# Layer 1's third couple: seven factor products over two pairs in place of eight block products, with the weight preparation moved ahead

## Chip, cores and metric

One Trainium2 chip, one core. The metric is the device time of one execution in microseconds (us), median of three runs. All matrix data is fp32; the kernel splits each operand into a high part (the value rounded to fp32r by a copy) and a low part (the rest) and forms each product as high·high + low·high + high·low, so three matmuls stand for one.

## What is computed

```
kv  = einsum('bhsd,bhse->bhde', k, v)            # 8 batches, 8 heads, 576 tokens, width 64
out = einsum('bhsd,bhde->bhse', q, kv)
x   = out / sqrt(mean(out^2) + 1e-6) * g_norm     # -> (4608, 512)
h   = x @ w_in;  x = (h * sigmoid(1.702 h)) @ w_out        # layer 1: 512 -> 2048 -> 512
h   = x @ w_in2; y = (s * relu(h)^2 + b) @ w_out2          # layer 2: 512 -> 2048 -> 512
```

## The kernel before

The 4608 tokens are nine tiles of 512; the 2048 hidden units are sixteen slices f of 128. Layer 1 of tiles 0, 1 and 2 runs first, in 48 "steps" (tile, f), by plain products: `mm1` (L587) makes one slice of h with 12 matmuls, `mm2` (L615) adds its share of the output two steps later with 12 more. Beside the steps, attention for later tiles is computed, layer 1's weights are unpacked from 64-bit words (`to_f32`, L155) and split, and `prep_first(p)` (L248) makes the weight factors that the next stage needs for w_in, from two slices at a time. It is a generator; `make()` advances it by one piece, three times at the end of each step (L1503), and one starts every fourth step from step 10 (L1196).

Then tiles go in couples of 1024 tokens: couples 0, 1, 2 are layer 1 of tiles 3 to 8, couples 3 to 6 are layer 2 of tiles 0 to 7, and tile 8 of layer 2 is last and alone. A couple has eight "pairs" P of two slices f; pairs 0 to 23 are layer 1, 24 to 55 layer 2. The first product of a pair is seven factor products i = 0 to 6 (`product`, L682; a "tick" is one of them), whose results are combined on the scalar and vector engines (`after`, L766).

The second product is done in two ways. In layer 1 `units` (L808) does, for each pair, eight block products ("unit": one token half t and one output block c) of six matmuls over 512 columns; the half t = 1 goes through a PSUM bank that the vector engine adds into SBUF (`z`, L840; one bank until pair 13, then two, L820), the half t = 0 stays in PSUM. The units of pair P-1 run between the products of pair P. In layer 2 a "quad" is two pairs: `quad_unit` (L974) does seven factor products in two halves h, one at each tick of the following two pairs, each of 12 matmuls over 256 columns; `factor_add`, `factor_hi` and `factor_lo` (L937, L959, L967) make the seven factors, `combine` (L1010) puts the results of a couple together when it has ended, and `load_t` (L867) loads the weight factors that `prep_out` (L270) stored. In the first two pairs of layer 2 no quad is there yet, so PE has only layer 1's last units and the first products.

Layer 2's weights are unpacked (`convert2`, L557) and turned into factors (`prep_in`, `prep_out`, L289 and L270) during the couples, as two tasks of a planner: at each tick `background` (L1250) advances tasks whose due tick has come, and others while the counted time of the vector and scalar engines leaves room. The due ticks are `14 + made2*4.6` and `18 + made2*4.6` (L1244), so the 32 slices end at about tick 161, pair 23. `parts_hl` (L225) splits a factor in a staging tile (`wst0`, `wst1`) and stores it to DRAM; `spaced` keeps two ticks between two of them.

All DMAs of these stages stand in SP's queue, in the order of the program.

Of the kernel before, what the change touches and what calls it, by code (L numbers as in the profile page):

```python
# [16 lines left out]
P = 128  # L17
# [27 lines left out]
ROOM = 500.0  # L45

# [6 lines left out]
def tile_attn_moe_moe2(  # L53
# [101 lines left out]
    def to_f32(which, ph, f):  # L155

        raw = w_raw.pop((which, ph, f))
        lo, hi = raw[:, :, 0], raw[:, :, 1]  # L160
        w = rot("wf", 3, (P, DM), U32)
# [58 lines left out]
    def spaced():  # L220
        while couples_on and now[0] < stored[0] + 2:
            yield 1
        stored[0] = now[0]

    def parts_hl(dst, src, n):  # L225

        yield
        yield from spaced()
# [4 lines left out]
        if isinstance(dst, list):  # L233
            for x, part in enumerate(dst):
                move(part, t[:, x])
        else:
            move(dst, t)
# [29 lines left out]

    wt_dram = {}

    def prep_out(p):  # L270

        wa, wb = (w_raw.pop((1, 1, f)) for f in (2 * p, 2 * p + 1))
        if p == 0:
            wt_dram.update({x: dp.tile([P, 8, 2, 2, KP], F32, name=f"wt{x}") for x in range(KF // 4)})
        a, b = (x.rearrange("p (h e) -> p h e", h=2) for x in (wa, wb))
        d = wt_dram[p // 2][:, :, p % 2]
        c = new("wc", (P, 4, KP))
        tt = vector.tensor_tensor
# [5 lines left out]
        yield from parts_hl(d[:, 0:8:7], a, 2)  # L284
        yield from parts_hl(d[:, 1:3], c[:, 0:2], 2)
        yield from parts_hl(d[:, 3:5], c[:, 2:4], 2)
        yield from parts_hl(d[:, 5:7], b, 2)

    def prep_in(p):  # L289
        a, b = (w_raw.pop((0, 1, f)).rearrange("p (h e) -> p h e", h=2) for f in (2 * p, 2 * p + 1))  # L290
        d = wi_dram[1, p] = dp.tile([P, 8, 2, KP], F32, name=f"wi1_{p}")
        c = new("wc", (P, 4, KP))
        yield from sums_of(a, b, c)
        yield from parts_hl(d[:, 0:2], a, 2)
        yield from parts_hl(d[:, 2:4], c[:, 0:2], 2)
        yield from parts_hl(d[:, 4:6], c[:, 2:4], 2)
        yield from parts_hl([d[:, 7], d[:, 6]], b, 2)
# [235 lines left out]
    def split_x(s, i):  # L533

        lay, m, _ = couples[s]
        if i == 6 and s > first2:
# [18 lines left out]
    made2 = [0, 0]  # L555

    def convert2():  # L557

        for m, (which, f) in enumerate(order2):
            made2[0] = m  # L560
            while m >= made2[1] + 3:
                yield 1
            for n, _ in enumerate(to_f32(which, 1, f)):
                yield 1 if n == 0 else 0
            if m + 2 < len(order2):
                load_w(order2[m + 2][0], 1, order2[m + 2][1])
        made2[0] = len(order2)

    def prepare2():

        for m, (which, f) in enumerate(order2):
# [4 lines left out]
            yield from (prep_in, prep_out)[which](f // 2)  # L576
            made2[1] = m + 1
# [69 lines left out]
    P2 = first2 * (KF // 2)  # L647
    place_of = {}
# [53 lines left out]

    def width(P_):
        return couples[pairs[P_][0]][1]

    raws = {}
    def c_new(P_, e):

        if layer(P_):
            q_, m = (P_ - P2) // 2, width(P_)  # L710
# [33 lines left out]
    def g_hi(P_, e):  # L744

        if layer(P_):
            return
# [12 lines left out]
    def g_lo(P_, e):  # L760
        if layer(P_):
            return
# [96 lines left out]
    FACTORS = 7  # L859
# [3 lines left out]
    quads = [(s_, x) for s_ in range(first2, LAST) for x in range(KF // 2 // BY)]  # L863
    t_t, f_t, mid_t, m_ps, m_sb = {}, {}, {}, {}, {}
    t_next = [0]

    def load_t():  # L867
# [3 lines left out]
        if n < len(quads) * FACTORS:  # L871
            q_, k_ = divmod(n, FACTORS)
            t = t_t[q_, k_] = new(f"wo{n % T_RING}", (P, 2, 2, KP), F32R)
            move(t, wt_dram[quads[q_][1]][:, k_])
        elif n < len(quads) * FACTORS + KF - 2:
            load_last(n - len(quads) * FACTORS, f"wo{n % T_RING}")

    def load_last(f, tag):
        t = t_t["last", f] = new(tag, (P, 2, 2, KP), F32R)
        move(t, wt_dram[f // 4][:, (slice(0, 8, 7), slice(5, 7))[f % 2], f // 2 % 2])  # L880
# [93 lines left out]
    def quad_unit(q_, k_, h):  # L974
# [13 lines left out]
        for c in range(2):  # L988
# [21 lines left out]
    def combine(s, h):  # L1010
# [4 lines left out]
        def send(k_, t, right):  # L1015
            row = js[0] * BT + t * m + 2 * h * P
# [49 lines left out]
    def load_wo2():  # L1066
# [4 lines left out]
        if n < first2 * KF:  # L1071
# [86 lines left out]
    for x, slot in ((0, 2), (0, 2), (0, 5), (0, 5), (1, 5)):  # L1158
        at((P2 + x, slot), "load", load_t)
# [35 lines left out]
    for p in range(KF // 2):  # L1195
        todo.setdefault(10 + 4 * p, []).append((prep_first, p))  # L1196
# [9 lines left out]
    for m in range(2):  # L1206
        at(len(steps) - 3 + m, "raw", load_w, 0, 1, m)
# [16 lines left out]
    def plan():  # L1224
# [3 lines left out]
        for s_ in range(len(couples)):  # L1228
            n0 = n * s_
            need = []  # L1230
            if s_:
                if couples[s_][0]:
                    need = [Task(y_get(s_), n0 - n + 6, n0 - n + 7)]
                if s_ < LAST:
                    need = [Task(fac_sums(s_), n0 - (14 if s_ <= first2 else 35), n0 - 9, need)]
            for i in range(7 if s_ < LAST else 2):
                if (s_, i) in split_early:
                    continue
                more = [split[s_, 1]] if (i == 6 and s_ <= first2 and (s_, 1) in split) else []
                split[s_, i] = Task(split_x(s_, i), max(0, n0 - 7 + i + 1), max(0, n0 + i - (4 if i < 6 else 5)), need + more)  # L1240
            if first2 <= s_ < LAST:
# [17 lines left out]
    with tc.manual_schedule():  # L1259
# [204 lines left out]

        split_early = [(0, i) for i in range(4)]
# [6 lines left out]
        for n in range(FIRST, N1):  # L1472
            conv = to_f32(*convs.pop(n)) if n in convs else iter(())
            start(n)
            run(n, "splith")
# [9 lines left out]
            run(n, "pe")  # L1485
            next(conv, None)
# [7 lines left out]
            next(conv, None)  # L1494
            y_out(n - 2, 2)
# [7 lines left out]
            make()  # L1503
            make()
            make()
            if n == N1 - 5:
                load_half(0)
# [38 lines left out]
        for P_, (s_, p) in enumerate(pairs):  # L1546
            lay, m, js = couples[s_]
            for i in range(7):
# [4 lines left out]
                at_q = ((P_ - P2) // BY, 7 * (P_ % BY) + i)  # L1553
                after(P_, i)
                if lay:
# [16 lines left out]
                elif i == 2 and layer(P_ - 1) == 0:  # L1572
                    running.append(units(P_ - 1))
                for _ in range({6: 2}.get(i, 1) if P_ < P2 else 1 if P_ == P2 or i % 2 == 0 else 0):
# [3 lines left out]
                if lay:  # L1578
# [3 lines left out]
                background(tick, slot, SLACK, ROOM if lay and P_ > P2 + 1 else 9999.0)  # L1582
# [87 lines left out]
```

## Time and profile before

| | |
|---|---|
| median of three runs | 1584.61 us (1583.83 to 1585.3) |
| the profiled execution, its own time | 1585.22 us |
| span of its profile | 1583.5 us |
| TensorE (PE) busy | 1563.4 us, 99% |
| VectorE (DVE), ScalarE (ACT) busy | 1001.3 us, 63% and 937.4 us, 59% |
| moved by DMA | 372.71 MB, mean 235 GB/s |

Engines are PE (matmul), PEld (its weight loads), DVE, ACT, POOL and SP. PE's busy time counts pipelined matmuls whose shown duration (0.39 us) is longer than their spacing, so the time of a stretch is read from start to start. The steps lie at 26 to 323 us of the span, pairs 0 to 15 at 323 to 682, pairs 16 to 23 at 682 to 846, layer 2's pairs 24 and 25 at 846 to 879, its other pairs up to 1471, and the lone tile at the end.

### The profile page before, as it was taken

The numbers are of one execution on the slowest core, as the hardware profiler recorded it, in microseconds if no ns is written. First come the engines' busy times: TensorE is split into PE (matmuls) and PEld (weight loads), VectorE is DVE, ScalarE is ACT, GpSimd is POOL, SyncE is SP. The second block draws the span as 40 slices with busy tenths as digits, with TensorE's granted clock in tenths as the row PEclk, the third lists the DMA queues.
The fourth block names the chain that finished last, engine by engine and source line by source line (L and its number), as shares of the span: only waits on it lengthen the run. The fifth ranks groups of instructions, "written<-read, shape, count | busy, mean of one in ns | idle before, by whom it ended". The sixth has DMA issues, their size and how long they took to land.

```text
span 1583.5 us, 23132 instructions
## 1 busy us (share of the span) xinstructions
PE 1563.4 (99%) x8880; PEld 1338.7 (85%) x8880; DVE 1001.3 (63%) x1478; ACT 937.4 (59%) x1520; POOL 69.3 (4%) x49
## 2 busy tenths in 40 slices
PE   7999999999999999999999999999999999999999
PEld 6788888878887888888888899899999998999987
DVE  6877743456666666777885466866686668556620
ACT  4766643454445555464446866776677677766652
POOL 4000111101000010000000000000000000000000
PEclk9999999999999999999999999999999999999999
DMA  8678877567776876789975755685568556755563
GB/s 279 199 265 308 274 259 258 199 207 244 272 240 231 293 255 219 248 278 362 357 282 199 253 188 186 213 268 189 185 216 263 188 188 210 241 193 184 189 219 113
DMA packets 127039, 372.71 MB, mean 235 GB/s; under 512 B 12626, under 2 KB 29266, under 8 KB 119762
## 3 DMA queue, kind: packets, MB, share of 16 engines
q1 hardware_dynamic: 126786, 371.12, 69.6%
q8 instruction: 70, 1.15, 0.3%
q14 instruction: 39, 0.32, 0.1%
q10 hardware_dynamic: 144, 0.13, 0.0%
HBM read 289.41 MB, written 81.79 MB: 234 GB/s over the span
## 4 chain that ended last, share of the span: by engine, by line
PE 90%; DVE 5%; ACT 2%; DMA 2%; issue 1%; SPq 0%; POOL 0%; DVEq 0%; ACTq 0%; POOLq 0%
PE A L696 6%; PE A L697 6%; PE A L698 6%; PE m L995 4%; PE m L994 4%; PE m L993 4%; PE D L696 3%; PE D L697 3%; PE D L698 3%; PE sum L830 3%; PE sum L832 3%; PE sum L831 3%; PE acc L624 3%; PE acc L625 3%; PE z L830 3%; PE acc L626 3%
## 5 line engine op out<-in xcount | busy, mean ns | idle before, releaser
L995 PE MATMUL m<-wo,fac 128*128 128x256 f32 x640 | 180.8, 283 | 0.6 <-DVE fac L89 0.6
L994 PE MATMUL m<-wo,fac 128*128 128x256 f32 x640 | 180.7, 282 | 0.0
L993 PE MATMUL m<-wo,fac 128*128 128x256 f32 x640 | 180.0, 281 | 0.0
L89 ACT ACTIVATE gh<-gh 128x512 f32<-128x512 f32 x72 | 45.4, 632 | 145.3 <-DVE gh L89 145.2
L994 PEld LDWEIGHTS m<-wo,fac 128*128 128x128 f32 x640 | 122.2, 191 | 6.1
L993 PEld LDWEIGHTS m<-wo,fac 128*128 128x128 f32 x640 | 121.2, 189 | 7.0
L995 PEld LDWEIGHTS m<-wo,fac 128*128 128x128 f32 x640 | 121.2, 189 | 1.2 <-DVE fac L89 1.2
L696 PE MATMUL A<-wi,xl 128*128 128x512 f32 x296 | 117.5, 397 | 1.9 <-ACT ev L89 0.7
L697 PE MATMUL A<-wi,xl 128*128 128x512 f32 x296 | 116.2, 393 | 0.0
L698 PE MATMUL A<-wi,xl 128*128 128x512 f32 x296 | 115.2, 389 | 0.0
L89 DVE TENSOR_TENSOR madd<-m,madd 128x512 f32<-128x512 f32 x122 | 83.8, 688 | 49.4 <-PE m L995 49.4
L89 ACT ACTIVATE wraw<-wraw 128x512 uint32<-128x512 uint32 (+1 forms) x128 | 82.7, 646 | 52.6 <-DVE wraw L89 52.6
L425 POOL TENSOR_TENSOR r<-ms,mhalf 128x8 f32<-128x8 f32 x36 | 65.6, 1826 | 544.0 <-DVE ms L89 543.9
L89 DVE TENSOR_TENSOR fac<-s,fac 128x1024 fp32r<-128x1024 f32 x64 | 77.9, 1218 | 15.0 <-ACT fac L89 15.0
L89 ACT ACTIVATE g<-h 128x512 f32<-128x512 f32 x52 | 31.0, 597 | 79.8 <-PE h L598 69.6
L596 PE MATMUL h<-xh,wi 128*128 128x512 f32 x192 | 76.5, 399 | 1.2 <-ACT g L89 1.2
L830 PE MATMUL z<-wo,wo 128*128 128x512 f32 x192 | 76.1, 396 | 1.2 <-DVE g L89 0.7
L624 PE MATMUL acc<-gh,wo 128*128 128x512 f32 x192 | 76.7, 399 | 0.0
L625 PE MATMUL acc<-gh,wo 128*128 128x512 f32 x192 | 75.1, 391 | 0.7 <-DVE wo L89 0.7
L626 PE MATMUL acc<-gl,wo 128*128 128x512 f32 x192 | 75.0, 390 | 0.0
L598 PE MATMUL h<-xl,wi 128*128 128x512 f32 x192 | 74.9, 390 | 0.0
L832 PE MATMUL z<-wo,wo 128*128 128x512 f32 x192 | 74.9, 390 | 0.0
(264 smaller groups left out, 4370.7 us busy)
## 6 DMA issues: line engine op xcount, KB each, us to landing
wo<-wt SPq DMA_DIRECT2D x127, 512.0 KB, 4.0
wo<-wo SPq DMA_DIRECT2D x80, 512.0 KB, 5.1
xl<-wi SPq DMA_DIRECT2D x37, 1024.0 KB, 6.5
xl<-wi SPq DMA_DIRECT2D x37, 768.0 KB, 5.9
wi<-wst SPq DMA_DIRECT2D x40, 512.0 KB, 4.5
xh<-wi SPq DMA_DIRECT2D x19, 1024.0 KB, 6.7
wraw<-in_w_in SPq DMA_DIRECT2D x32, 512.0 KB, 4.1
wraw<-in_w_out SPq DMA_DIRECT2D x32, 512.0 KB, 4.4
```

What stands on the lines that cost most here:

```text
L89: return fn(*args, **kw)
L624: nc.tensor.matmul(o, wh[:, ds_], gh, start=(f == lo), stop=False)
L625: nc.tensor.matmul(o, wl[:, ds_], gh, start=False, stop=False)
L626: nc.tensor.matmul(o, wh[:, ds_], gl, start=False, stop=(f == hi - 1))
L696: nc.tensor.matmul(o, wh, xh, start=(c == 0 and not more), stop=False, skip_group_check=more)
L697: nc.tensor.matmul(o, wl, xh, start=False, stop=False, skip_group_check=more)
L698: nc.tensor.matmul(o, wh, xl, start=False, stop=(c == 1), skip_group_check=more)
L830: nc.tensor.matmul(o, wh[:, cs], gh, start=begins, stop=False)
L832: nc.tensor.matmul(o, wh[:, cs], gl, start=False, stop=ends)
L993: nc.tensor.matmul(o[:, c, :], hi[:, y, cs], w[:, y, 0, :], start=begins, stop=False)
L994: nc.tensor.matmul(o[:, c, :], hi[:, y, cs], w[:, y, 1, :], start=False, stop=False)
L995: nc.tensor.matmul(o[:, c, :], lo[:, y, cs], w[:, y, 0, :], start=False, stop=ends)
```

## The change

- Couple 2 (pairs 16 to 23) does its second product in quads. Four quads of layer 1 come before the sixteen of layer 2. A layer 1 factor product has the weights standing and the 512 tokens moving: six matmuls over 512 columns for each half h. `c_new`, `g_hi`, `g_lo`, `factors`, `beside_quads` and `combine` take these pairs as they took layer 2's; the two pairs without a quad are now 16 and 17.
- `prep_first_out(p)`, eight of them from step 33 on, make the w_out factors for layer 1 and store them. `prep_first` starts at steps 10, 14, 18, 21, 24, 26, 28, 30; from step 21 `make()` is called four times in a step, two of them in its middle.
- Layer 2's weight preparation: the first raw loads six steps earlier; 14 advances of `convert2` in steps 41 to 47; then due ticks by small steps, `7 + (steps2[0]-15)*0.66` and `8 + steps2[1]*0.68`, so it ends at about tick 106, pair 15. Converting may be four slices ahead (three before).
- Staging: the stores leave at the next tick; a staging tile may be taken again after three ticks, at most one a tick, and `f5` is a third tile in ticks 4 to 40 and 60 to 96.
- The planner's room for DVE is 1300 ns a tick up to pair 17 (9999 before), 500 after.
- Couple 3 makes its seventh factor in places of its own, as couples 4 to 6 do, and its sums may start earlier.

```diff
+REUSE = 3
+F5_TAKEN = ((-99, 3), (41, 59), (97, 999))
...
-        t = rot("wst", 2, (P, 2, 2, KP), F32R)[:, 0:n]
+        t = (yield from staging())[:, 0:n]
...
-            move(dst, t)
+        stores.append((dst, t))
+        if not couples_on and not 33 <= now[0] < len(steps) - 5:
+            store()
...
+    def prep_first_out(p):
+        if p % 2 == 0:
+            wt_dram[0, p // 2] = dp.tile([P, FACTORS, 2, 2, KP], F32, name=f"wt0_{p // 2}")
+        d = wt_dram[0, p // 2][:, :, p % 2]
+        ab = new("f5", (P, 2, 2, KP))
+        for x in range(2):
+            parts = [part.rearrange("p (h e) -> p h e", h=2) for part in w_out[0, 2 * p + x]]
+            for y, part in enumerate(parts):
+                if x == 0:
+                    move(d[:, 0, y, :], part[:, 0, :])
+                else:
+                    move(d[:, 5:7, y, :], part)
+            vector.tensor_tensor(out=ab[:, x], in0=parts[0].bitcast(F32), in1=parts[1].bitcast(F32), op=ALU.add)
+        yield
+        c = new("wc", (P, 4, KP))
+        yield from out_sums(ab[:, 0], ab[:, 1], c)
+        yield from parts_hl(d[:, 1:3], c[:, 0:2], 2)
+        yield from parts_hl(d[:, 3:5], c[:, 2:4], 2)
...
-            while m >= made2[1] + 3:
+            while m >= made2[1] + 4:
...
+    firstq = first2 - 1
+    PQ = firstq * (KF // 2)
...
-    quads = [(s_, x) for s_ in range(first2, LAST) for x in range(KF // 2 // BY)]
+    quads = [(s_, x) for s_ in range(firstq, LAST) for x in range(KF // 2 // BY)]
...
+        for y in range(BY) if couples[s][0] == 0 else ():
+            hs = slice(h * P, (h + 1) * P)
...
+            nc.tensor.matmul(flat, w[:, y, 0, hs], hi[:, y, :], start=begins, stop=False)
+            nc.tensor.matmul(flat, w[:, y, 1, hs], hi[:, y, :], start=False, stop=False)
+            nc.tensor.matmul(flat, w[:, y, 0, hs], lo[:, y, :], start=False, stop=ends)
...
-        todo.setdefault(10 + 4 * p, []).append((prep_first, p))
+        todo.setdefault((10, 14, 18, 21, 24, 26, 28, 30)[p], []).append((prep_first, p))
+    for p in range(KF // 2):
+        todo.setdefault(33 + 7 * p // 4, []).append((prep_first_out, p))
...
-        at(len(steps) - 3 + m, "raw", load_w, 0, 1, m)
+        at(len(steps) - 9 + m, "raw", load_w, 0, 1, m)
...
-        Task(convert2(), 7, lambda: 14 + made2[0] * 4.6)
-        Task(prepare2(), 5, lambda: 18 + made2[1] * 4.6)
+        Task(converting, 6, lambda: 7 + (steps2[0] - 15) * 0.66)
+        Task(prepare2(), 7, lambda: 8 + steps2[1] * 0.68)
...
+            if n >= N1 - 7:
+                for _ in range(2):
+                    next(converting)
...
-                background(tick, slot, SLACK, ROOM if lay and P_ > P2 + 1 else 9999.0)
+                background(tick, slot, SLACK, ROOM if P_ > PQ + 1 else 1300.0)
```

## Rows read from the trace of the kernel before

**Rows 1.** The page: busy time of the engines, and the chain that ended last.
```profile
PE 1563.4 (99%) x8880; PEld 1338.7 (85%) x8880; DVE 1001.3 (63%) x1478; ACT 937.4 (59%) x1520; POOL 69.3 (4%) x49
PE 90%; DVE 5%; ACT 2%; DMA 2%; issue 1%; SPq 0%; POOL 0%; DVEq 0%; ACTq 0%; POOLq 0%
```
**Rows 2.** Windows by stage: from:to, us, busy of each engine, clock, DMA share, GB/s.
```profile
224.30:280.60 56.30, 55.13 (x378) 45.41 (x376) 18.75 (x36) 19.29 (x37) 8.82 (x5) 1.00 0.75 248
280.60:322.60 42.00, 42.00 (x203) 34.97 (x201) 17.81 (x25) 18.50 (x32) 6.20 (x3) 1.00 0.59 202
322.60:501.40 178.80, 176.20 (x950) 142.68 (x949) 115.97 (x196) 91.41 (x166) 14.63 (x8) 1.00 0.71 239
501.40:682.30 180.90, 179.78 (x905) 147.30 (x904) 124.60 (x212) 93.57 (x169) 13.82 (x8) 1.00 0.75 256
682.30:845.50 163.20, 163.20 (x721) 135.14 (x721) 128.61 (x204) 83.08 (x146) 0.00 (x0) 1.00 0.85 308
845.50:879.00 33.50, 32.85 (x145) 26.85 (x144) 13.53 (x17) 20.60 (x33) 0.00 (x0) 1.00 0.72 262
1018.30:1451.00 432.70, 432.31 (x2769) 392.61 (x2768) 284.75 (x333) 306.67 (x453) 0.00 (x0) 1.00 0.65 214
```
**Rows 3.** PE's timeline: first matmuls of two units 512 columns wide.
```profile
727.23 0.39 PE L830 MATMUL sum<-wi,wo 128*128 128x512 f32 x1
...
729.95 0.39 PE L830 MATMUL z<-wo,wo 128*128 128x512 f32 x1
```
**Rows 4.** PE's timeline: a layer 2 factor product, and the matmul after it.
```profile
1060.84 0.28 PE L993 MATMUL m<-wo,fac 128*128 128x256 f32 x1
...
1062.27 0.40 PE L696 MATMUL A<-wi,xl 128*128 128x512 f32 x1
```
**Rows 5.** What PE waited for, 320 to 682 us: total us, times, longest.
```profile
PE xtp L435 <- DVE xn L89: 0.8, 2, 0.6
PE z L830 <- DVE g L89: 0.7, 2, 0.6
PE A L696 <- ACT ev L89: 0.7, 1, 0.7
```
**Rows 6.** What PE waited for, whole span: layer 2's start, quads, mm2.
```profile
PE acc L625 <- DVE wo L89: 0.7, 2, 0.5
...
PE A L696 <- ACT wst L89: 0.7, 1, 0.7
PE m L995 <- DVE fac L89: 0.6, 3, 0.2
```
**Rows 7.** Groups by line, whole span: weight preparation on DVE and ACT.
```profile
L89 DVE TENSOR_SCALAR wf<-wf 128x512 f32<-128x512 f32 (+1 forms) x128 | 54.1, 423 | 13.4 <-ACT wf L89 12.3
...
L89 DVE TENSOR_TENSOR wst<-wc,wst 128x512 fp32r<-128x512 f32 x48 | 32.5, 685 | 2.1 <-ACT wst L89 2.1
...
L89 ACT CAST wst<-wc 128x512 fp32r<-128x512 f32 x48 | 29.6, 616 | 12.5 <-DVE wc L89 5.4 <-DMA wt<-wst 3.9 <-DMA y<-ev 1.7
...
L89 DVE TENSOR_TENSOR wc<-wf 128x256 f32<-128x256 f32 x32 | 13.3, 417 | 0.0
```
**Rows 8.** Windows, DVE on wf tiles alone: pairs 0 to 15, 16 to 23.
```profile
322.60:682.30 359.70, 74.22 (x144) 1.00 0.73 248
682.30:845.50 163.20, 41.37 (x80) 1.00 0.85 308
```
**Rows 9.** Windows, all engines: steps 24 to 28.
```profile
166.60:198.20 31.60, 31.37 (x154) 26.08 (x153) 22.57 (x43) 19.98 (x36) 4.12 (x2) 1.00 0.80 273
```
**Rows 10.** Windows, all engines: pair 18.
```profile
723.10:743.50 20.40, 20.40 (x91) 16.89 (x91) 12.95 (x24) 10.57 (x20) 0.00 (x0) 1.00 1.01 394
```
**Rows 11.** DMA issues from 682 to 800 us: KB each, median us to landing.
```profile
f<-y SPq DMA_DIRECT2D x15, 512.0 KB, 7.6
```
**Rows 12.** DMA issues from 322 to 682 us: stores of staged factors.
```profile
wt<-wst SPq DMA_DIRECT2D x20, 512.0 KB, 3.8
```
**Rows 13.** What SP's queue waited for, 320 to 682 us.
```profile
SPq L125 <- DVE wst L89: 103.9, 29, 8.3
```

More of the change, by code (lines that the diff above doesn't have):

```diff
@@ L218, in tile_attn_moe_moe2, with staging @@
     now, stored = [0], [-9]
-    def spaced():
-        while couples_on and now[0] < stored[0] + 2:
+    used = {"wst0": -99, "wst1": -99, "f5": -99}
+    def staging():
+        if not couples_on:
+            turns["wst"] = turns.get("wst", -1) + 1
+            places = ("wst0", "xh1", "xl1") if 33 <= now[0] < len(steps) - 5 else ("wst0", "wst1")
+            return new(places[turns["wst"] % len(places)], (P, 2, 2, KP), F32R, "wst")
+        while True:
+            free = [x for x in used if now[0] - used[x] >= REUSE and (x != "f5" or not any(lo <= now[0] <= hi for lo, hi in F5_TAKEN))]
+            if free and now[0] > stored[0]:
+                x = min(free, key=used.get)
+                used[x] = stored[0] = now[0]
+                return new(x, (P, 2, 2, KP), F32R, "wst")
             yield 1
-        stored[0] = now[0]
     def parts_hl(dst, src, n):
         yield
-        yield from spaced()
-        t = rot("wst", 2, (P, 2, 2, KP), F32R)[:, 0:n]
+        t = (yield from staging())[:, 0:n]
         scalar.copy(t[:, :, 0, :], src)
@@ L232, in parts_hl, with store @@
         vector.tensor_tensor(out=t[:, :, 1, :], in0=src, in1=t[:, :, 0, :].bitcast(F32), op=ALU.subtract)
[L233 to L236, printed above, removed]
-            move(dst, t)
+        stores.append((dst, t))
+        if not couples_on and not 33 <= now[0] < len(steps) - 5:
+            store()
+    stores = []
+    def store():
+        while stores:
+            dst, t = stores.pop(0)
+            if isinstance(dst, list):
+                for x, part in enumerate(dst):
+                    move(part, t[:, x])
+            else:
+                move(dst, t)
     def sums_of(a, b, c):
@@ L575, in prepare2 @@
                 continue
-            yield from (prep_in, prep_out)[which](f // 2)
-            made2[1] = m + 1
+            for wait in (prep_in, prep_out)[which](f // 2):
+                steps2[1] += wait != 1 or stored[0] == now[0]
+                yield wait
     steps = [(j, f, lo, hi) for j, lo, hi in PARTS for f in range(lo, hi)]
@@ L701, in layer, with quad @@
         return couples[pairs[P_][0]][0]
+    def quad(P_):
+        return P_ >= PQ
     def width(P_):
@@ L707, in c_new @@
     def c_new(P_, e):
-        if layer(P_):
-            q_, m = (P_ - P2) // 2, width(P_)
+        if quad(P_):
+            q_, m = (P_ - PQ) // 2, width(P_)
             if (q_, e) not in raws:
@@ L744, in g_hi @@
     def g_hi(P_, e):
-        if layer(P_):
+        if quad(P_):
             return
@@ L760, in g_lo @@
     def g_lo(P_, e):
-        if layer(P_):
+        if quad(P_):
             return
@@ L858, in tile_attn_moe_moe2 @@
     BY = 2
-    FACTORS = 7
     T_RING = 5
@@ L987, in quad_unit @@
             o = m_ps[key]
-        for c in range(2):
+        for y in range(BY) if couples[s][0] == 0 else ():
+            hs = slice(h * P, (h + 1) * P)
+            begins = y == 0 and (first or not held(q_, k_))
+            ends = y == BY - 1 and (last or not held(q_, k_))
+            flat = o.rearrange("p a b -> p (a b)")
+            nc.tensor.matmul(flat, w[:, y, 0, hs], hi[:, y, :], start=begins, stop=False)
+            nc.tensor.matmul(flat, w[:, y, 1, hs], hi[:, y, :], start=False, stop=False)
+            nc.tensor.matmul(flat, w[:, y, 0, hs], lo[:, y, :], start=False, stop=ends)
+        for c in range(2) if couples[s][0] else ():
             cs = slice((2 * h + c) * P, (2 * h + c + 1) * P)
@@ L1156, in tiles_in @@
             at((P_, 3 * e + 3), "pre", x_raw, i + e)
-    for x, slot in ((0, 2), (0, 2), (0, 5), (0, 5), (1, 5)):
-        at((P2 + x, slot), "load", load_t)
+    for x, slot in ((0, 2), (0, 2), (0, 5), (1, 4), (1, 5)):
+        at((PQ + x, slot), "load", load_t)
     at(n0 + 10, "load", load_q, 5 * TT)
@@ L1485, in tile_attn_moe_moe2 @@
             run(n, "pe")
+            for _ in range(0 if n < 21 else 1):
+                make()
             next(conv, None)
@@ L1494, in tile_attn_moe_moe2 @@
             next(conv, None)
+            for _ in range(0 if n < 21 else 1):
+                make()
             y_out(n - 2, 2)
@@ L1502, in tile_attn_moe_moe2 @@
             run(n, "load")
-            make()
-            make()
-            make()
+            for _ in range(3 if n < 21 else 2):
+                make()
+            if n >= N1 - 7:
+                for _ in range(2):
+                    next(converting)
             if n == N1 - 5:
+                store()
                 load_half(0)
@@ L1571, in tile_attn_moe_moe2 @@
                             y_out(N1 - 1, d)
-                elif i == 2 and layer(P_ - 1) == 0:
+                elif i == 2 and not quad(P_ - 1):
                     running.append(units(P_ - 1))
-                for _ in range({6: 2}.get(i, 1) if P_ < P2 else 1 if P_ == P2 or i % 2 == 0 else 0):
+                for _ in range({6: 2}.get(i, 1) if P_ < PQ else 1 if P_ == PQ or i % 2 == 0 else 0):
                     while running and next(running[0], StopIteration) is StopIteration:
```

57 lines of the change are left out of this document (38 added, 19 removed), and 2 rows, old and new, of the table PLACES.

## Prediction

> **What bounds the kernel now.** I read the page first. PE is busy for 99% of the span, and the chain that ended last runs through PE for 90% [rows 1]. So the time is PE's work plus the few microseconds in which it waits, and a change pays only by taking matmuls away or gives back by making PE wait. Next the timeline, for what a matmul costs: from the first matmul of a unit at 727.23 to that of the unit after next at 729.95 lie twelve matmuls 512 columns wide, 2.72 us, 0.2267 us each [rows 3]. Then the windows: pairs 16 to 23 last 163.2 us, 20.40 a pair [rows 2]. A pair has 42 matmuls of first products and 48 of units, and 90 x 0.2267 = 20.40: in couple 2 PE loses nothing at all today. Last the waits: in pairs 0 to 15 PE waited on DVE and ACT for little more than these 2.2 us [rows 5], and elsewhere behind the start for single ones, DVE's `wo`, ACT's `wst` and DVE's `fac` [rows 6]. The reader is to see a PE that is full, with a DVE that is busy 65%, 69% and 79% of pairs 0 to 7, 8 to 15 and 16 to 23 [rows 2].
>
> **The second product of couple 2.** Removed: 8 pairs x 8 units x 6 = 384 matmuls of 512 columns. Added: 4 quads x 7 factors x 2 halves x 6 = 336 of the same width. So 48 x 0.2267 = 10.9 us leave PE [rows 3]. A pair should go from 20.40 to 84 x 0.2267 = 19.04 us. For a check from another shape, layer 2's factor half takes 1.43 us for twelve matmuls of 256 columns [rows 4], and its pairs 432.7 / 22 = 19.67 us [rows 2]; the wide form, six at 0.2267 = 1.36 us, is a little cheaper. [...]
>
> **The edge.** The two pairs without a quad last 33.5 us today [rows 2], for 144 matmuls = 32.6, with one wait of 0.7 us on ACT [rows 6]. They move from 24 and 25 to 16 and 17 with the same content: 0. Pairs 24 and 25 then carry the last layer 1 quad and `combine`. Layer 2's couples pay at this place one wait each, three in all for 0.6 us, on DVE's `fac` [rows 6]; with the slowing that follows I add 0.4 us, between 0 and 1.
>
> **DVE in pairs 16 to 25.** Out go 32 additions of z, 32 low parts of g and the preparation; in come, per quad, four additions and seven low parts on 1024 elements and ten additions from PSUM. Layer 2 has the same load and DVE is busy 66% there [rows 2], with these small waits; ACT has no squares to make in layer 1. The fetching of couple 3's four partial sums stays here with its due ticks. I take 0 for it, and 2 us as the worst.
>
> **The preparation, moved ahead.** On wf tiles DVE spent 74.2 us in pairs 0 to 15 and 41.4 in 16 to 23 [rows 8]; `wst<-wc` adds two thirds of 32.5 = 21.7 us in all [rows 7], 7.8 of them late in the same proportion. So 49 us come forward. Some 6 us of it (14 advances, not three slices, at 2 x 0.42 + 2 x 0.69 us) go to steps 41 to 47; 43 us are added to the 240.6 us of pairs 0 to 15, which makes 284 of 359.7 us, 79% [rows 2, 7]. That is just what DVE had in pairs 16 to 23, where PE lost nothing [rows 2]. But from pair 13 z has two banks and before that one, with a single product of 1.36 us between two z units: there a late DVE stops PE at once, as it did twice today [rows 5]. The bounds: nothing or even 2 us less, since the room of 1300 ns spreads DVE's work and the known waits are accidents of order; 10 us, if each of the 13 pairs with one bank has one wait like the longest today, 0.6 to 0.8 us. I take 1.5 us, near the low end, because the row nearest in load (pairs 16 to 23) shows none. What waits behind DVE: ACT's gelu and copies, which need its sums, and through them PE's bank for A.
>
> **The steps.** Each `prep_first_out` costs DVE 4 x 0.685 + 4 x 0.417 = 4.4 us [rows 7], 35 us in all, and ACT two copies of 0.62. Steps 33 to 47 have 36.6 us of DVE in 98.3 [rows 2]; with 35 more, 6 of conversion, and two `prep_first` gone earlier (-9), 69, or 70%. Crowded is the end: in the last 42 us DVE has 17.8, and 3.4 of the eight preparations and the conversion add 21: 39 of 42. Steps 24 to 28 go from 22.6 of 31.6 us to 27 with one more `prep_first` [rows 9]. Today's waits on DVE's split of `wo` are 0.7 us for two [rows 6]. `mm2` runs two steps behind `mm1`, so a lateness of one step is covered; if that cover is gone, each microsecond of surplus is one of PE. Bounds 0 and 5 us (the surplus a step-long burst could reach); I take 1.5.
>
> **DMA.** `prep_first_out` has six DMAs, 1.8 MB, 14.7 MB in all, of which two moved `prep_first` give back 3.7 in steps 33 to 47: 228 GB/s become some 340 [rows 2]. Pairs 0 to 15 get 36% of 50 MB, 50 GB/s more, some 300. Pair 18 today has 394 GB/s with its engines full, and still lasts 20.40 us [rows 10]; transfers then land in 7.6 us [rows 11], against loads that are issued two steps (11 us) or more ahead. So 0. Couple 2 reads 28 factor tiles in place of 48 - 32 = 16 `wo` tiles of the same size, while the preparation's traffic has left: less than today's 308 GB/s [rows 2]. The raw loads moved to steps 39 and 40 and the five `load_t` moved to pairs 16 and 17 go where their places are free. SP's queue loses a wait: it stood 103.9 us behind DVE's `wst` in pairs 0 to 15 [rows 13], and stores now leave a tick later. Loads behind it leave earlier, which PE, that waits for no load, does not feel: 0.
>
> **The sum.** 1585.2 us of the profiled execution - 10.9 + 0.4 + 1.5 + 1.5 = 1577.7. The median lies 0.6 below that execution, so 1577.1; rounded, 1577.
>
> **Rivals.** (1) *Nothing new waits*, and some of today's small waits go: 1584.6 - 10.9 - 0 to 2 = 1571.5 to 1574. For it: a DVE load that PE has borne [rows 2]; against it, two crowded places at once.
>
> (2) *DVE's lateness eats the saving.* The single z bank and the last steps cost 8 to 13 us, the upper bounds of both: 1581.5 to 1588. For it: the wait exists already [rows 5]; against it, it is 0.7 us now.
>
> (3) *Slower: ACT stands before a staging tile.* Copy at tick t, subtraction at t+1, store at t+2 or later, landing 3.8 us after it [rows 12], or 7.6 where DMA is full [rows 11]: t+3.4 to t+4.8 at 2.72 us a tick, and the tile may be taken at t+3. Before, the store left a tick earlier and the tile came back after four. While f5 is taken (ticks 41 to 59 and 97 to 106) only two tiles turn, for some 16 stores, one in 1.75 ticks. Each can hold ACT for 1.1 to 4.9 us, 18 to 78 in all, and behind it stand the copies that empty PE's banks. A bank has some 3 us of cover (three groups of 1.36 less a copy). It decides where the mean wait is 0.9 us above that cover: 16 x 0.9 = 14 us, and the kernel is at 1588 or more. Against it: ACT waited 3.9 us for such stores in the whole run [rows 7], and the oldest tile is taken first. [...]
>
> (4) *The preparation does not end by pair 15*, as it waits for tiles: couple 2 then finds `wraw` and `wst` taken, and its first quad waits for the rest, some 2 to 6 us: near 1581. I count it with (2).
>
> **Chances.** Forecast, 1574 to 1581.4: 0.55. Rival 1: 0.17. Rival 2 with 4: 0.16, of which 0.13 lie within 0.2% (3.2 us, about what tells a change of this kernel from none: 1581.4 to 1587.8) and 0.01 below it. Rival 3: 0.12. So faster 0.73, same 0.13, slower 0.14. The range for 8 in 10 is 1572 to 1586; the forecast's own is 1574 to 1581.
>
> **What would show it.** 48 matmuls fewer; pairs 18 to 25 at 19.0 us; 33.5 us for pairs 16 and 17; DVE near 79% of pairs 0 to 15, with the waits of z on DVE at 1 to 3 us; the last 42 us of the steps longer by 1 to 2 us. Wrong would be: waits of `A` on ACT behind `wst` in pairs 6 to 8 and 14, 15; a lower clock (it is full throughout [rows 2]); quads of 512 columns with longer spacing than 0.2267; PE waiting on a DMA.

## The result: slower, and the loss lies where only preparation was added

Median of four executions 1595.38 us (1594.42 to 1595.88) against 1584.62 us (1583.83 to 1585.3) for the kernel before in the same comparison: a ratio of 1.0067, 95% interval 1.005 to 1.0085. The forecast was 1577, range 1572 to 1586; the time lies beyond both.

The page after, busy time and chain, to set beside [rows 1]:

```profile
PE 1560.2 (98%) x8832; PEld 1329.7 (83%) x8832; DVE 1066.9 (67%) x1568; ACT 957.9 (60%) x1539; POOL 69.5 (4%) x49
PE 82%; DVE 8%; ACT 4%; DMA 3%; issue 2%; SPq 0%; POOL 0%; DVEq 0%; ACTq 0%; POOLq 0%
```

The 48 matmuls are gone, 8880 to 8832. But the chain, which ran 90% through PE, is now 18% outside it: PE has work to wait for. Where, the windows by stage of the kernel after say (columns as in [rows 2]: steps; pairs 0 to 15; pairs 16 to 25; the last 42 us of the steps):

```profile
24.80:323.50 298.70, 293.26 (x1644) 241.27 (x1642) 215.14 (x401) 172.78 (x309) 30.22 (x17) 1.00 0.84 294
323.50:699.50 376.00, 360.80 (x1853) 289.73 (x1851) 278.52 (x486) 204.23 (x373) 29.92 (x16) 1.00 0.81 284
699.50:888.20 188.70, 187.15 (x817) 152.92 (x817) 133.77 (x154) 94.18 (x138) 0.00 (x0) 1.00 0.73 252
281.50:323.50 42.00, 42.00 (x203) 34.96 (x202) 34.56 (x63) 25.48 (x45) 5.30 (x3) 1.00 0.96 362
```

| stage | before, us | after, us | difference | forecast |
|---|---|---|---|---|
| first matmul of the steps | 26.0 | 24.8 | -1.2 | 0 |
| 48 steps | 296.6 | 298.7 | +2.1 | +1.5 |
| pairs 0 to 15 | 359.7 | 376.0 | **+16.3** | +1.5 |
| pairs 16 to 25 | 196.7 | 188.7 | -8.0 | -10.5 |
| the rest | 704.4 | 705.8 | +1.4 | 0 |

The first and the last line are not the change's: with unchanged code they vary from 23.6 to 26.7 and from 704.2 to 706.0 over the runs below. Each line is one execution; the steps, for one, last 298.7 to 300.4 us in the runs below that leave them as they are after the change. What is left is one loss of 16.3 us in pairs 0 to 15, where PE's program is what it was and only DVE, ACT and SP have more to do.

What waited there, by the waits of 326 to 705 us after (total us, times, longest), beside [rows 5]:

```profile
DVE ms L91 <- ACT xn L91: 38.4, 16, 4.9
ACT wst L91 <- DMA wt<-wst: 21.4, 8, 5.3
...
ACT wst L91 <- DMA wi<-wst: 13.4, 5, 4.8
...
DVE wst L91 <- ACT wst L91: 6.3, 5, 2.2
...
PE xtp L486 <- DVE xn L91: 3.7, 5, 1.4
...
PE z L889 <- DVE gl L91: 3.1, 2, 2.5
...
PE u L458 <- ACT f L91: 2.7, 3, 1.5
...
PE z L889 <- DVE g L91: 2.1, 1, 2.1
...
PE D L752 <- ACT gh L91: 1.4, 2, 1.0
```

Three things are to be seen. PE's waits add up to 14.9 us, with four short ones of 1.9 that are left out here; before they were 3.5 in these pairs. Of the 16.3 us, 11.4 are thus longer waits; 1.7 more, an estimate from the granted clock, are a lower clock behind one of them (last section), and the other 3.2 are not broken down here. ACT now stands 34.8 us, 13 times, before a staging tile whose last store has not landed; before, it never did in these pairs, and for 6.1 us in the whole run, 3.9 of them in the group of [rows 7]. And DVE stands 38.4 us with attention's row sums (`ms`) at the head of its queue, waiting for ACT's squares; that is old, 34.8 us before.

The loss is not spread: against before, pair 8 is 3.9 us longer, pair 7 3.4, pair 1 2.5, pair 5 2.1, pair 10 1.5, pair 4 1.1, the others under 1. Pair 7, by the timelines of ACT, of DVE and of PE (start, duration, engine, line, operation; in brackets the idle time before it and what ended it):

```profile
500.65 0.62 ACT L91 CAST wst<-wc 128x512 fp32r<-128x512 f32 x1 [3.56 <-DMA wi<-wst]
501.18 0.58 ACT L91 COPY gh<-D 128x512 f32<-128x512 f32 x1
```
```profile
501.30 0.69 DVE L91 TENSOR_TENSOR wst<-wc,wst 128x512 fp32r<-128x512 f32 x1 [2.23 <-ACT wst L91]
...
502.49 0.42 DVE L91 TENSOR_TENSOR wc<-wf,wc 128x256 f32<-128x256 f32 x1
...
505.23 0.68 DVE L91 TENSOR_TENSOR gl<-z,gl 128x512 f32<-128x512 f32 x1
```
```profile
501.81 0.50 PE L752 MATMUL D<-wi,xh 128*128 128x512 f32 x1 [1.03 <-ACT gh L91]
505.97 0.50 PE L889 MATMUL z<-wo,wo 128*128 128x512 f32 x1 [2.50 <-DVE gl L91]
```

A store that had not landed held ACT's copy 3.56 us; behind it stood the copy that empties D, and PE waited 1.03 for that bank. DVE, at its subtraction, waited 2.23 for the same copy; then came four sums, a split and another addition, and only at 505.23 the one that frees z's one bank. PE waited 2.50 for it. One late store cost PE twice, by two engines.

Pair 8 is another kind, DVE's timeline and PE's:

```profile
521.89 0.68 DVE L91 TENSOR_TENSOR g<-z,g 128x512 f32<-128x512 f32 x1
522.49 0.68 DVE L91 TENSOR_TENSOR wst<-wc,wst 128x512 fp32r<-128x512 f32 x1
...
523.66 0.43 DVE L91 TENSOR_TENSOR wc<-wc,wf 128x256 f32<-128x256 f32 x1
...
527.21 0.69 DVE L91 TENSOR_TENSOR g<-z,g 128x512 f32<-128x512 f32 x1
```
```profile
527.95 0.50 PE L889 MATMUL z<-wo,wo 128*128 128x512 f32 x1 [2.08 <-DVE g L91]
```

DVE waits for nothing here. It has run without a gap since 511.6, and between two additions of z it does 4.6 us of other work, a subtraction, four sums, two splits of couple operands and two conversion steps. z's bank is wanted again sooner than that.

### The profile page after: what moved, and what is told of

It reads as the page before. It is cut to its first block, busy times and chain, and to the rows that moved or that the text cites. A ratio compares the mean times of both kernels' runs of the same rounds, so it can differ in the third digit from the quotient of the medians.

```text
span 1594.1 us, 23281 instructions
## 1 busy us (share of the span) xinstructions
PE 1560.2 (98%) x8832; PEld 1329.7 (83%) x8832; DVE 1066.9 (67%) x1568; ACT 957.9 (60%) x1539; POOL 69.5 (4%) x49
## 4 chain that ended last, share of the span: by engine, by line
PE 82%; DVE 8%; ACT 4%; DMA 3%; issue 2%; SPq 0%; POOL 0%; DVEq 0%; ACTq 0%; POOLq 0%
PE A L752 6%; PE A L753 5%; PE A L754 5%; PE m L1064 4%; PE m L1063 4%; PE m L1062 4%; PE D L752 3%; PE D L753 3%; PE D L754 3%; PE acc L678 2%; PE acc L679 2%; PE acc L680 2%; PE h L650 2%; PE h L652 2%; PE h L651 2%; DVE wf L91 2%
## 5 line engine op out<-in xcount | busy, mean ns | idle before, releaser
L91 DVE TENSOR_TENSOR madd<-m,madd 128x512 f32<-128x512 f32 x152 | 104.4, 687 | 58.3 <-PE m L1064 49.5
L91 ACT ACTIVATE wraw<-wraw 128x512 f32<-128x512 f32 (+1 forms) x136 | 88.0, 647 | 71.3 <-DVE wraw L91 71.1
L91 DVE TENSOR_TENSOR fac<-s,fac 128x1024 fp32r<-128x1024 f32 x80 | 97.4, 1217 | 17.0 <-ACT fac L91 17.0
L91 ACT CAST fac<-s 128x1024 fp32r<-128x1024 f32 x80 | 83.5, 1044 | 0.0
L91 ACT ACTIVATE wi<-wi 128x512 f32<-128x512 f32 x72 | 45.3, 630 | 54.7 <-DVE wi L91 54.7
L650 PE MATMUL h<-xh,wi 128*128 128x512 f32 x192 | 76.5, 399 | 1.7 <-ACT g L91 1.7
L91 ACT ACTIVATE gh<-gh 128x512 f32<-128x512 f32 x48 | 30.2, 630 | 75.4 <-DVE gh L91 75.2
L651 PE MATMUL h<-xh,wi 128*128 128x512 f32 x192 | 74.8, 389 | 0.0
```

What stands on the lines that cost most here:

```text
L91: return fn(*args, **kw)
L650: nc.tensor.matmul(o, wh[:, cs], xh[:, c, :], start=(c == 0), stop=False)
```

## The experiments

Times are medians with the ratio to before and its 95% interval; before was run again beside each group of runs, 1584.56 to 1585.15 us. "Pairs 0 to 15" is that stage's length in the one profiled execution, 359.7 before and 376.0 after.

| | edit to the kernel after | us | ratio | pairs 0 to 15 |
|---|---|---|---|---|
| x1 | store at once | 1591.96 | 1.0044 [1.0027, 1.006] | 372.8 |
| x2 | tile again after 4 ticks | 1586.28 | 1.0014 [1.0005, 1.0023] | 365.7 |
| x3 | couple 2 in units | 1601.16 | one execution | 374.4 |
| x4 | lighter conversion | 1587.93 | 1.0022 [1.0013, 1.0031] | 366.2 |
| x8 | x2 and x4 | 1579.96 | one execution | 359.6 |
| x5 | x2, tasks start earlier | 1595.65 | 1.007 [1.0055, 1.0085] | 375.0 |
| x6 | x2, row sums a tick later | 1580.74 | 0.9975 [0.9965, 0.9985] | 360.6 |
| x7 | x5 and x6 | 1587.69 | 1.0018 [1.0009, 1.0027] | 368.9 |
| x11 | row sums a tick later alone | 1589.48 | 1.0029 [1.0019, 1.004] | 370.7 |
| x10 | the same in the kernel before | 1583.48 | 0.9991 [0.9982, 1.0] | 359.0 |
| x9 | x6, all `prep_first` spread | 1584.74 | 0.9997 [0.9988, 1.0006] | 359.5 |
| x12 | x6, one `prep_first` a step earlier | 1579.65 | 0.9963 [0.995, 0.9977] | 359.9 |

The theories were: the staging tiles (ACT before a store), DVE's load in the crowded pairs, and for x3 that the quads themselves carry a cost.

**x1, the stores leave at once.**
```diff
-        if not couples_on and not 33 <= now[0] < len(steps) - 5:
-            store()
+        store()
```


> One part undone: each staged factor is stored as soon as its low part is made, not at the next tick. Two theories for the 16 us that pairs 0 to 15 gained (359.7 to 376.0 us). Staging: ACT stands 35 us before staging tiles whose store has not landed (6 us before the change), and what it would do next comes late. Then the earlier stores bring ACT's waits on stores under 20 us, pairs 0 to 15 to 366 to 371 us and the time to 1585 to 1591 us. Load: DVE has 49 us more in-order work in these pairs and everything behind it is late, whoever waits for a store. Then ACT's waits on stores fall too, but the pairs stay above 373 us and the time at 1592 to 1597 us.

ACT's waits for stores fell from 34.8 us to 10.7, pair 7 from 24.9 to 22.6, and pair 14 lost its 0.7. Pair 8 stayed at 28.0 and pairs 1 to 5 did not move. The time lies between the two forecasts. So the 24 us of waiting for stores that went were worth some 3 of the 16 us. It was neither the whole cause nor nothing.

**x2, a tile may be taken again after four ticks.**
```diff
-REUSE = 3
+REUSE = 4
```


> A staging tile may be taken again after four ticks, not three. Staging theory: ACT's waits on stores fall from 35 to under 12 us, pairs 0 to 15 take 364 to 370 us, the time is 1584 to 1590 us. Load theory: the waits fall, but the same work stands in DVE's queue and partly later; pairs 0 to 15 stay at 373 to 378 us, the time at 1592 to 1598 us.

10.3 us come back, yet ACT still waits 21.7 us for stores, more than in x1: what this constant does is not only to let stores land. Pairs 7 and 8 in the windows of x2, and in DVE's timeline the same two additions of z and the second of four sums, twice:

```profile
490.40:510.80 20.40, 20.40 (x91) 16.85 (x90) 17.08 (x27) 13.17 (x22) 0.00 (x0) 1.00 0.89 290
510.80:535.00 24.20, 24.20 (x171) 19.23 (x170) 22.52 (x38) 14.12 (x25) 0.00 (x0) 1.00 0.84 314
```
```profile
513.99 0.43 DVE L91 TENSOR_TENSOR wc<-wf,wc 128x256 f32<-128x256 f32 x1
...
520.13 0.69 DVE L91 TENSOR_TENSOR g<-z,g 128x512 f32<-128x512 f32 x1 [0.43 <-PE z L891]
...
523.81 0.69 DVE L91 TENSOR_TENSOR g<-z,g 128x512 f32<-128x512 f32 x1 [0.46 <-PE z L891]
...
531.99 0.43 DVE L91 TENSOR_TENSOR wc<-wc,wf 128x256 f32<-128x256 f32 x1
```

Pair 8 has DVE busy 93% and PE loses nothing. The second of four sums reads `wc,wf` for a w_in factor and `wf,wc` for a w_out factor, which tells the pieces apart. The piece that stood between the two additions (523.66 after, 12 us into pair 8) now comes 21 us into the pair, behind both; the piece before it, in pair 7 after (502.49), now opens pair 8. From the end of the first addition to the other lie 3.0 us, and DVE waits for PE. So `REUSE` also sets in which tick a piece of preparation is made, here a later one, and in pair 8 that is what counts.

**x3, couple 2 back in units, all else as after** (the edits that give couple 3 its own places are undone with it).
```diff
-    firstq = first2 - 1
+    firstq = first2
```


> One part undone: couple 2 does its second product in eight block products as before, and all else of the change stays (the layer 1 factors are made and stored but not used). Both theories: pairs 0 to 15 stay at 374 to 378 us, pairs 16 to 25 take 196 to 198 us in place of 188.7, so the time is 1602 to 1606 us. If the quads themselves cost something outside their pairs, it is lower, under 1600 us.

Pairs 16 to 25 are 196.8 us, as before, and the whole is 1601.16, just under the 1602 to 1606 of both theories. The quads are worth 8.1 us in their pairs; the rest of the change costs some 16. Pairs 0 to 15, with the same work for DVE and ACT as after, took 374.4 against 376.0, and pairs 7 and 8 25.2 and 25.6 against 24.9 and 28.1. So single executions can differ by 2 us in this stage and by more in a pair, and a cost of the quads elsewhere of that size can't be seen.

**x4, two conversion steps on DVE less for each slice of layer 2**, the planner's count kept. The kernel leaves out what limits, shifts and masks the unpacked words, so layer 2 gets wrong weights.
```diff
-        vector.tensor_scalar(
...
+        if ph == 0:
+            vector.tensor_scalar(
...
+        else:
+            clock["dve"] += 75 + DM * 1.04 / 2
```


> Layer 2's weights are unpacked without their two TENSOR_SCALAR instructions, so that layer 2 works with wrong weights; the planner still counts them and the rest of the order stays. DVE has 64 x 0.42 = 27 us less, some 24 of it in pairs 0 to 15. Load theory: more than half of the 16 us goes, pairs 0 to 15 take 363 to 368 us, the time is 1582 to 1588 us. Staging theory: ACT still stands before the staging tiles for 30 us or more, pairs 0 to 15 stay above 371 us, the time is 1590 to 1595 us.

**x8, x2 and x4 together.**


> Staging tiles reused after four ticks, and layer 2's weights unpacked without their two TENSOR_SCALAR instructions (so layer 2 works with wrong weights). If staging and load are the two causes and nothing else: pairs 0 to 15 are back at 358 to 362 us (before: 359.7) and the time is near 1577 to 1580 us. If a third cause is left: 364 us or more, 1583 us or more.

The windows of pairs 0 to 15, x4 and then x8:

```profile
322.70:688.80 366.10, 357.73 (x1853) 289.26 (x1851) 255.35 (x427) 204.10 (x373) 30.22 (x16) 1.00 0.83 291
```
```profile
324.20:683.80 359.60, 355.69 (x1854) 290.09 (x1853) 255.69 (x428) 205.55 (x374) 30.27 (x16) 1.00 0.85 296
```

With 23 us of DVE work less the stage is 9.9 us shorter although ACT waits 38.2 us for stores, more than after. DVE's load is thus a cause, and not the waits alone. With both edits the stage is as long as before (359.6): load and the rule on tiles explain the loss. Whether they add is not decided. In the stage each takes 10 away and both 16.4; but x4's profiled execution was its fastest, 1585.13, so its stage may be longer in the median. By the medians, each against before beside it, x2 takes 9.1 us from the change's loss, x4 7.5 and both (one execution) 15.4.

**x5, the tasks start at tick 1 and are paced to the same end**, so that the same work is thinner.
```diff
-        Task(converting, 6, lambda: 7 + (steps2[0] - 15) * 0.66)
-        Task(prepare2(), 7, lambda: 8 + steps2[1] * 0.68)
+        Task(converting, 1, lambda: 2 + (steps2[0] - 15) * 0.69)
+        Task(prepare2(), 1, lambda: 3 + steps2[1] * 0.715)
```


> Staging tiles reused after four ticks, and layer 2's preparation may begin at tick 1 of pair 0 (not 6 and 7) and is due in correspondingly gentler steps up to the same end. Pair 0 has only 9.5 us of DVE work in 20.5 us, pairs 1 to 5 have 19 to 21 in 24. Load theory (what is left after four ticks, in pairs 1 to 5, is DVE's and ACT's queue being too full): pairs 1 to 5 lose 2 to 5 of the 6.6 us that they are longer than before, 1581 to 1585 us. Rival (what is left comes from the order around attention, whatever the load): under 1 us, 1585 to 1588 us.

The time lies above both forecasts. Waits for stores fell to 8.9 us, from 21.7 in x2, and the kernel is as slow as after. Pair 0, which had room, now loses 2.7 us to a wait of A on ACT, and pair 9 has the longest wait of all, in PE's timeline:

```profile
554.49 1.16 PE L458 MATMUL u<-kvbd,q 128*128 128x128 f32 x8 [3.95 <-ACT f L91]
```

In the 14 us ahead of it ACT stood 2.5 us for a store and 2.1 for `gh`; which of them decides was not tried. It shows again that few waits for stores do not make a fast kernel.

**x6, x2 with attention's row sums one tick later**, so that ACT's squares are ready when DVE comes to them.
```diff
-            at((P_, 3 * e), "post", att_r, i + e)
+            at((P_, 3 * e + 1), "pre", att_r, i + e)
```


> Staging tiles reused after four ticks, and in pairs 1, 2, 4, 5 and 9 to 12 the row sums of the squares for attention stand one tick later in DVE's queue, so that DVE does not stand before ACT's square (35 us in all, 15 times) with its other work behind it. If DVE's standing time counts as load just as its work does: that wait falls under 15 us, the pairs with attention lose 3 to 6 us, 1580 to 1584 us. Rival: the norm, now a tick nearer to its sums, is late in their place and PE's transposes wait for DVE as long or longer: 1586 to 1590 us.

**x11, the same line alone, `REUSE` 3.**


> The change with the row sums one tick later and staging tiles still reused after three. If staging and DVE's standing are two separate losses: pairs 7 and 8 still take some 49 to 53 us (the change: 53.0; four ticks: 44.7), pairs 1 to 5 fall as they did with both edits, from 121.7 to some 117 to 118, pairs 0 to 15 take 369 to 372 us, the time is 1588 to 1592 us. If relieving DVE cures the staging waits too: under 365 us, 1585 us or less.

**x10, the same line in the kernel before.**


> The kernel before with the row sums one tick later and nothing else. If DVE's standing before ACT's square cost only because the change filled DVE: the kernel before gains less than 1.5 us (its transposes waited 0.8 us for DVE in pairs 0 to 15), 1583 to 1585 us. If it was a loss of the kernel before as well: 2 us or more, under 1582.6 us.

In all three runs the first forecast held: 1580.74, 1589.48 and 1583.48 us. The chain that this line cuts, in the kernel after, pair 5, by the timelines of DVE, ACT and PE:

```profile
444.88 0.69 DVE L91 TENSOR_REDUCE ms<-xn 128x8 f32<-128x512 f32 x1 [3.74 <-ACT xn L91]
...
448.54 0.68 DVE L91 TENSOR_TENSOR gh<-B,gh 128x512 f32<-128x512 f32 x1
```
```profile
449.26 0.63 ACT L91 ACTIVATE gh<-gh 128x512 f32<-128x512 f32 x1 [4.41 <-DVE gh L91]
...
453.44 0.84 ACT L91 ACTIVATE f<-xtp,g 128x256 f32<-128x256 f32 x2
```
```profile
454.34 1.16 PE L458 MATMUL u<-kvbd,q 128*128 128x128 f32 x8 [1.46 <-ACT f L91]
```

DVE stood 3.74 us before the row sums; behind them lay 2.9 us of conversion and splitting, then `gh`. ACT's gelu stood 4.41 us for `gh`, seven more instructions followed on ACT, then `f`, and PE waited for `f`. In these rows nothing passes the sums: DVE starts nothing in the 3.74 us before them, ACT nothing in the 4.41 us before the gelu. With the sums a tick later this wait leaves DVE's list altogether; in x11 DVE stands before PE's `B` for 18.6 us (3.9 after), so it is early there. Pairs 1, 4 and 5 fall from 24.1, 24.3 and 25.3 to 22.3, 23.2 and 23.2, while 37.7 us of waits for stores stay, with pairs 7, 8 and 12 at 25.3, 25.6 and 27.4 (after: 24.9, 28.1, 24.7). So it is a loss of its own: 5.3 us in pairs 0 to 15. From there, four ticks in place of three take away 10.1 more (370.7 to 360.6), as they took 10.3 in x2. These two add, by the medians too: 6.3 and 9.1 us, together 14.6. Behind x2, then, either the later sums (x6) or the lighter conversion (x8) gives back about the rest. In the kernel before the same line is worth 0.7 us of the stage (1.5 by the medians), and its interval touches 1: the standing time was there already and cost little; what made it cost was the work queued behind it.

**x7, x5 and x6 together.**


> Both edits together over the four ticks. If each takes its own waits: 1577 to 1582 us, pairs 0 to 15 in 358 to 362 us. If both take the same waits: no better than the better of the two, 1581 to 1584 us.

Neither forecast held. 368.9 stands against 360.6 with the tasks at their old start: the early start costs 8.3 us here and 9.3 between x2 and x5.

**x9, x6 with `prep_first` at steps 10, 13, 17, 20, 22, 27, 29, 31**, so that steps 24 to 28 have less.
```diff
-        todo.setdefault((10, 14, 18, 21, 24, 26, 28, 30)[p], []).append((prep_first, p))
+        todo.setdefault((10, 13, 17, 20, 22, 27, 29, 31)[p], []).append((prep_first, p))
```


> Four ticks, the row sums a tick later, and layer 1's w_in factors started at steps 10, 13, 17, 20, 22, 27, 29, 31 (the change: 10, 14, 18, 21, 24, 26, 28, 30), which leaves steps 25 and 26 free of them. The waits of mm2 on DVE's split of wo in steps 16, 26 and 27 were 2.7 us with the four ticks and the later sums; if they come from this work standing before the splits, they fall to 1 us or less, the steps to 297 to 298 us and the time to 1578 to 1580 us. If they come from the unpacking alone: no change, 1580 to 1581 us.

The waits on `wo` left steps 26 and 27 (from 7.95 and 7.57 us in x6 to 6.37 and 6.28), but step 35 went to 12.8, from 7.1, and the time, 1584.74 us, lies above both forecasts. PE's waits there, the windows behind them, and in ACT's timeline and the chain that ended last what came before:

```profile
PE kvps L385 <- DMA kv<-in_v: 2.3, 1, 2.3
PE kvps L385 <- ACT gh L91: 1.5, 1, 1.5
```
```profile
246.00:248.00 2.00, 2.00 (x7) 1.51 (x6) 0.00 (x0) 0.62 (x1) 0.00 (x0) 0.50 1.04 404
248.00:252.00 4.00, 4.00 (x16) 3.25 (x15) 2.04 (x4) 0.00 (x0) 0.00 (x0) 0.82 1.07 399
```
```profile
233.74 1.08 ACT L91 COPY ev<-acc 128x512 f32<-128x512 f32 x2 [3.74 <-DMA wi<-wst]
```
```profile
238.86 5.59 DMA kv<-in_v
```

The same load in SP's timeline of x6:

```profile
238.50 0.43 SPq L366 DMA_DIRECT2D kv<-in_v  x1
```

PE waited for a value tile of attention. Its transfer was not slow: 5.6 us to landing, where the same loads have a median of 5.5 in pairs 0 to 15 of the kernel after. It left late, 1.9 us behind the first matmul of step 35 (at 236.98 us), in x6 2.7 us ahead of it (at 241.20 us). ACT had stood 3.74 us until the store of a w_in factor, from a `prep_first` that now starts later, had landed; its copies of the accumulators were late by it, and in SP's queue their stores stand ahead of attention's loads. x2 has the same wait once, with 0.7 us, and no other run has it. Attention's loads of these steps are not far ahead of their use.

**x12, x6 with one of the eight a step earlier.**
```diff
-        todo.setdefault((10, 14, 18, 21, 24, 26, 28, 30)[p], []).append((prep_first, p))
+        todo.setdefault((10, 14, 18, 21, 23, 26, 28, 30)[p], []).append((prep_first, p))
```


> Four ticks, the row sums a tick later, and one w_in factor of layer 1 started at step 23 in place of 24, the others as in the change, so that their end (step 32) does not move and nothing is put beside the key and value loads of steps 33 to 35. If the waits of mm2 in steps 26 and 27 (1.9 us) come from this factor's work standing before the split of wo: the steps lose 1 us, 1579 to 1580.5 us. If not: 1580.5 to 1581.5 us, like four ticks and later sums alone.

Its windows of steps and pairs 0 to 15:

```profile
25.40:323.60 298.20, 293.24 (x1644) 241.27 (x1643) 215.06 (x401) 172.99 (x309) 30.27 (x17) 1.00 0.85 295
323.60:683.50 359.90, 356.11 (x1854) 289.95 (x1853) 278.63 (x487) 206.39 (x374) 28.70 (x16) 1.00 0.85 296
```

Waits on `wo` went from 2.7 us in x6 to 1.7, and the steps from 299.3 to 298.2, by the 1 us that was forecast for this cause. But the intervals of the two runs overlap, so that the time gains by it is not shown; both kernels are faster than before, x12 by 5.5 us. Pairs 0 to 15 have 278.6 us of DVE work, the same as after, in 359.9 us in place of 376.0.

Not varied alone were the planner's room of 1300 ns, the third staging tile and the DMA traffic (284 GB/s in pairs 0 to 15, 248 before); what share they have in the loss stays open.

## Why the prediction was wrong, by its own steps

**"The preparation, moved ahead" is the step that failed.** It put 1.5 us on it, within 0 (or a gain of 2) and 10, and it was 16.3. The amount of work was right: DVE was forecast 284 us in these pairs and has 278.5. The conclusion was not. It took the low end because pairs 16 to 23 carry the same 79% and lose nothing, and the runs show why that row was no model. Pairs 16 to 23 have two banks for z and no attention. In pairs 0 to 15 DVE stands at the head of its queue for ACT: 34.8 us for the row sums, which is in no busy share, and what it does afterwards comes in bursts. x11 measures what this costs under the new load, 5.3 us. The second part is the order in time: a share over 360 us says nothing of the 4.6 us between two additions of z in pair 8. The upper bound, one short wait for each pair, assumed waits no longer than the old ones; they came to 2.5 us.

**Rival 3, ACT before a staging tile, was right in its mechanism and too cheap a chance.** In pair 7 the copy that empties D does come behind a wait of 3.56 us for a store. Waits of 34.8 us lie within its 18 to 78. It was held to be unlikely because ACT waited 3.9 us in the run before (6.1 with all groups, none of it in pairs 0 to 15), where the rule for taking a tile was another and only 45 store transfers went out in pairs 0 to 15 against 72 now. The landing time it used, 3.8 us [rows 12], is 6.1 after for the same kind of store. But its decision was wrong: PE's waits do not come from A alone, and waits for stores by themselves explain some 3 us (x1). The rule on tiles explains 10 (x2; x11 to x6); as x1 took away more of the waiting for 3 us, most of the 10 should come by the ticks into which the rule moves DVE's work. How the 10 divide between landing and moving can't be read exactly, since every change of the rule moves the work; pair 7, which x1 shortened by 2.3 us, is shown for the first, and pair 8, which only x2 cured of the two, for the second.

**So rivals 2 and 3 came together.** The prediction gave each a chance and no case to both, and its range ended at 1586, inside the times of rival 2 alone. They share the engines: a late store delays ACT, ACT delays DVE's subtraction, and DVE comes late to z.

**The quads.** Forecast -10.5 with the edge, measured -8.0. The content was right, 48 matmuls fewer and 33.6 us for pairs 16 and 17, forecast 33.5. The slowing behind a wait, which the 0.4 us of the edge counts, is in PE's timeline of the kernel before: behind the wait of 0.20 us on `fac` at 1010.40 the next matmul starts 0.23 us later, the ones after it 0.12 apart. The spacing was not that of units everywhere. PE's timeline of a quad's half:

```profile
740.08 0.40 PE L1054 MATMUL m<-fac,wo 128*128 128x512 f32 x1
740.32 0.40 PE L1055 MATMUL m<-fac,wo 128*128 128x512 f32 x1
740.55 0.39 PE L1056 MATMUL m<-fac,wo 128*128 128x512 f32 x1
```

In every other factor product (six of the first quad's fourteen halves) two of three matmuls stand 0.235 to 0.237 us from the next, not 0.227, so pairs 18 to 22 last 19.16 to 19.29 us, not 19.04, and pairs 24 and 25 19.4. They are the products whose factor lies in the places `wc` and `wo5`; `factor_hi` takes these by turns with `wo6` and `wo7`. Whether the place is the reason was not tried. And pair 23 is 20.2 us: two copies for couple 3 were queued ahead on ACT, in the timelines of ACT and PE,

```profile
846.97 1.99 ACT L91 CAST wi<-f 128x1024 fp32r<-128x1024 f32 x2
848.87 0.58 ACT L91 ACTIVATE xh<-A 128x512 f32<-128x512 f32 x1
```
```profile
849.50 0.50 PE L752 MATMUL A<-wi,xh 128*128 128x512 f32 x1 [0.87 <-ACT xh L91]
```

and PE waited 0.87 for a bank of A. The forecast put nothing on couple 3's sums there.

**The steps** were right in size, +2.1 for a forecast of +1.5 (up to +3.8 in the other runs), but not in place. The crowded last 42 us (DVE 34.6, forecast 39) last 42.0 as before, with DMA at 362 GB/s and no wait of PE. The loss is three waits on `wo`, 2.2 us against 0.7 [rows 6], two of them in steps 26 and 27, in which DVE was busy for 7.1 of 7.2 and 7.5 of 7.6 us, and 0.5 us more in a wait of `h` on ACT's `g`, 1.7 against 1.2.

**DMA** was right for the change as it is: PE waits for no transfer in these stages. The reason was too wide. Not all loads are two steps or more ahead: the value tile that x9 shows left 2.7 us ahead of its step in x6. SP's wait behind DVE's `wst` did not vanish, it is 85.1 us against 103.9 [rows 13]: the store comes a tick later, and so does DVE.

**Rival 4** did not occur: the last store of the preparation leaves at 688.7, in pair 15, and PE waits for nothing in pair 16. The old wait of 0.7 us on ACT's `wst` moved to pair 17 with the edge.

## What to carry to other kernels

Before work is moved onto an engine because its busy share leaves room, add the time in which it stands at the head of its queue for another engine, and look at the work between two deadlines (here two additions of z), not at a share over a stage. A staging buffer's rule of reuse is part of the schedule: it sets when stores must have landed and also in which tick each piece is made, so try its number both ways. And when a saving is small (here 8 us of PE), ask which other stage pays for it: the same saving with two lines changed made the kernel faster instead of slower.

## What the runs showed of the hardware

A wait of PE was paid for again in pair 8. Behind the 2.08 us wait there, the windows of the kernel after:

```profile
527.90:529.50 1.60, 1.55 (x5) 1.26 (x6) 1.60 (x2) 0.10 (x1) 0.00 (x0) 0.74 0.55 198
529.50:532.00 2.50, 2.50 (x23) 1.72 (x23) 2.39 (x5) 2.26 (x5) 0.00 (x0) 0.50 1.02 291
532.00:535.00 3.00, 3.00 (x22) 2.20 (x22) 1.12 (x3) 1.17 (x2) 0.00 (x0) 0.98 0.99 393
```

PE was granted 0.74 and then 0.50 of its full clock, the latter for 2.5 us, and was back at 0.98 after that; three matmuls of z start at 528.81, 529.24 and 529.67 there, 0.43 us apart in place of 0.227. At those shares 1.6 and 2.5 us lose 0.4 and 1.25, 1.7 in all, an estimate; with the 2.2 us from the matmul before the wait to the one behind it, beyond their spacing, that is the 3.9 us by which pair 8 is longer. In x9, behind waits of 1.5 and 2.3 us, PE was granted 0.50 for 2 us and 0.82 for 4, which by the same estimate is 1.7 us lost again. In pair 7 waits of 1.0 and 2.5 us left the clock at 1.00 over the pair; which waits lower it, these runs don't settle. The lower clock is in the stage lengths above: pair 8 was granted 0.94 in the mean both after and in x1, matmuls of 512 columns start 0.43 us apart for 3.4 us behind the 3.95 us wait of x5, and the mean over pairs 0 to 15 is 0.99 in x7 and x11. It is 1.00 in x2, x4, x6, x8 and x12, but also after, where one stretch does not show in it.
